# Shorter loads for every ninth tile of attention, and the first expert's weights queued behind the attention's last load

## The chip, the cores and the metric

The kernel runs on one core of one Trainium2 chip. The metric is the device time of one execution, in microseconds (us). The kernel before takes 399.77 us, the median of three runs (399.61 to 401.5).

The engines are named as the profile names them: PE (TensorE, the matrix products), PEld (its weight loads, which overlap PE), DVE (VectorE), ACT (ScalarE), POOL (GpSimd) and SP (SyncE, which here only issues DMAs). SBUF is the memory on the chip, PSUM the banks that PE writes.

## The reference

Decayed attention without a softmax, and behind it a layer of experts of which each token uses at most one:

```python
scores = scale * np.matmul(q, k.transpose(0, 1, 3, 2))     # q, k, v: 8 x 8 x 576 x 64
Dmat   = np.where(rel >= 0, gamma[:, None, None] ** rel[None, :, :], 0.0)
attn   = np.matmul(scores * Dmat[None, :, :, :], v)
x      = attn.transpose(0, 2, 1, 3).reshape(4608, 512)

do_compute = x @ w_skip > 0
xc     = x[do_compute]
logits = xc @ w_gate                                       # 8 experts
e_idx  = np.argmax(logits, axis=1)
gate_w = softmax(logits)[np.arange(len(xc)), e_idx]
for e in range(8):
    h       = np.maximum(xc[e_idx == e] @ w1[e], 0.0)      # 512 -> 1024
    y[e_idx == e] = gate_w[e_idx == e, None] * (h @ w2[e]) # 1024 -> 512
out = x;  out[do_compute] = xc + y
```

## The kernel before

**Attention (about 0 to 156 us).** It goes over 36 tiles of 128 tokens (NT = 36, number g), nine (NQ) for each pair of sequences. The first eight of the nine hold 64 tokens of each of two sequences' blocks; the ninth (g % NQ == HALF, so g = 8, 17, 26, 35) holds the last 64 rows of both. A tile's input is one buffer `u_g` of four parts of 128x512 numbers: parts 0 and 1 are columns of q and k, part 2 rows of v, part 3 rows of k. There are UBUFS = 5 such buffers. `load_half(g, s)` (L501) fetches two parts by one 512 KB DMA on SP's queue: the first half (s = 0) of tile g+4 is written behind `values` of tile g-1, which frees the buffer (L852); the second half (s = 2) of tile g+3 a step later, behind the last product of a block on PE (L836).

For each tile PE makes `scores` (L552, results psc and psq in PSUM), DVE and ACT multiply them by the decays (`decay`, L573: sq at L578, u in place at L581, ACT's copy at L585), POOL multiplies the rows of k by a table (`keys`, L587: kn) and the rows of v by another (`rows_of`, L604: vs), PE makes the running state of a sequence from kn and u or vs (`state`, ps_s at L626) and the tile's result from scores and state (`values`, pxt at L651 and L675, which DVE scales into xt at L687). `stage_c` (L689) turns xt by PE into px; ACT copies it to xn and sends it to the output. `keys` returns at once for the ninth tile: a sequence's state isn't needed behind its last rows, so part 3 of tiles 8, 17, 26 and 35 is loaded and never read. Before the loop `keys(0)` stands twice (L788 and L822) and writes the same values.

**Routing.** Every four tiles, `logits_a` and `logits_b` make the gate logits (PE pl, ACT lt, PE pn, DVE lg at L717); px, pl and pn share one PSUM bank. `route_a` and `route_b` (DVE, L187 to L258) find each token's expert, gate weight and rank; `slot_match` (DVE r, L266) and `slot_add` (PE ps_m, L271) add them to the table of slots. This is done in six groups of tiles (GROUPS, 8 8 8 4 4 4). Behind the third, the first expert is chosen, and SP reads its number into a register (L359). Behind the fourth, `close_first` fixes the first 256 tokens of that expert (CUT); POOL gathers their rows by two indirect DMAs (xg, L341), and `turn_early` and `up_early` start this expert's first products (ph_early) while the last two groups are still being routed. DVE's rl (L405) belongs to the slots' table, which the experts' gathers need.

**The first expert's weights.** A chunk of weights is 512 KB. It is loaded into one of four raw buffers (tag "w", `load_w`, L157), and split into a rounded part and a rest: ACT casts whi, and a subtraction makes wlo. For the first expert's first five chunks (AHEAD = 5) this is `weights()` (L744): each call starts the load of the next chunk, n, and splits chunk n-2, with ACT's cast at L753 and POOL's subtraction in four pieces at L758. It is called at the end of each step g once the expert's register is there (from g = 29 on), and then in a loop behind the last tile until five chunks are split. All other chunks are split by `split_w` (ACT L169, DVE L170) in the experts' part.

**Experts (about 180 to 395 us).** PE multiplies almost without a pause.

The order on PE is written out by hand (`in_turn` interleaves the products of several steps); the order on the other engines is made by the scheduler from the order of the code, from when things are ready and from `add_manual_dep`, with the operations of `weights()` kept in program order.

Of the kernel before, what the change touches and what calls it, by code (L numbers as in the profile page):

```python
# [22 lines left out]
NTOK, DM, NE, DF = B * S, H * D, 8, 1024  # L23
P = 128
NT = NTOK // P
HALF = S // P * 2
NQ = HALF + 1
# [21 lines left out]
UAHEAD = UBUFS - LAG  # L49
# [36 lines left out]
def kernel(  # L86
# [10 lines left out]
    nc = tc.nc  # L97
# [15 lines left out]
    def keep_up(n):  # L113
        for _ in range(n):
            nc.tensor.matmul(ps_m, warm[:, :P], warm, start=True, stop=True)
# [41 lines left out]
    def load_w(e, f, regs):  # L157

        t = wpool.tile([P, 2, NCC, P], F32, tag="w", name=f"w_{e}_{f}", bufs=4)
        marks["load"] = nc.sync.dma_start(t.rearrange("p m c i -> p (m c i)"), w[bass.ds(regs[e], 1), f].rearrange("o p c -> (o p) c"))  # L160
        return t

    def parts(t):
        return [wpool.tile([P, 2, NCC, P], F32R, tag=n, name=f"{n}_{t.name}") for n in ("whi", "wlo")]
# [277 lines left out]
    wq, hs, marks = {}, {}, {}  # L442
    regs = []
# [38 lines left out]
    with ExitStack() as actx:  # L482
# [16 lines left out]
        u_t = {}  # L499

        def load_half(g, s, after=None):  # L501
            if s == 0:
                u_t[g] = ap.tile([P, 4, NPR, P], F32, tag="u", name=f"u_{g}", bufs=UBUFS)
            half = nc.sync.dma_start(
                u_t[g][:, s : s + 2].rearrange("p s a i -> p (s a i)"),
                qkv[g, s // 2],
            )
            if after is not None:
                tc.add_manual_dep(
                    half.ins,  # L510
                    after.name,
                    mybir.DependencyInfo(mybir.DependencyClass.Sync, mybir.DependencyReason.DATA),
                    reason="the second half begins behind a block of products",
                )
# [5 lines left out]
        def last_product():  # L520
            return next(i for i in reversed(nc.cur_bb.bb.instructions) if i.engine == mybir.EngineType.PE)
# [30 lines left out]
        def scores(g):  # L552

            u = u_t[g]
            psc_t[g] = [
                pp.tile([P, NPR, P], F32, tag=f"sc{g % 2}", name=f"psc_{g}"),
                pp.tile([P, NPR, D], F32, tag="sc2", name=f"psq_{g}"),
            ]
            for a in range(NPR):
                for c in range(2):  # L560
                    q = first(g) if c == 0 else slice(D, P)
                    for j in range(2):
                        nc.tensor.matmul(  # L563
                            psc_t[g][c][halves[1 - j ^ c], a, : q.stop - q.start],
                            u[halves[j], 1 - j, a, c * D : (c + 1) * D],
                            u[halves[j], j, a, q],
                            start=a == 0,
                            stop=a == NPR - 1,
                            skip_group_check=True,
                        )  # L570
                yield
# [15 lines left out]
        def keys(g):  # L587
            i = g % NQ
            if i == HALF:
                return  # L590
            kn_t[g] = ap.tile([P, NPR, P], F32, tag="kn", name=f"kn_{g}")
            k = TK + i // 2 * 2
            nc.gpsimd.tensor_tensor(  # L593
                kn_t[g].rearrange("p a (j i) -> p a j i", j=2),
                u_t[g][:, 3].rearrange("p a (j i) -> p a j i", j=2),
                tt_sb[:, k : k + 2, :].rearrange("p j a -> p a j").unsqueeze(3).broadcast_to([P, NPR, 2, D]),
                ALU.mult,
            )
# [44 lines left out]
        def second(g):  # L643

            last = g % NQ == HALF
            px_t[g] = pp.tile([P, NPR, P], F32, tag="xt", name=f"pxt_{g}", bufs=2)
            for a in range(NPR):
                for n in range(1 + last):
                    for j in range(2):
                        h = halves[j]  # L650
                        nc.tensor.matmul(  # L651
                            px_t[g][h, a, D:],
                            st_t[g][h, a, :] if n else u_t[g][h, 2, a, j * D : (j + 1) * D],
                            u_t[g][h, j, a, D:] if n else sc_t[g][h, a, :],
                            start=a == 0 and n == 0,
                            stop=False,
                            skip_group_check=True,
                        )
                yield

        def in_turn(*products):

            products = list(products)
            while products:
                products = [p for p in products if next(p, p) is not p]
# [76 lines left out]
        chunks = []  # L742

        def weights():  # L744

            if not regs:
                return
            n = len(chunks)
            chunks.append(None)
            if 0 <= n - 2 < AHEAD:  # L750
                t = chunks[n - 2]
                hi, lo = wq[0, n - 2] = parts(t)
                tc.keep_in_program_order(nc.scalar.copy(hi, t))  # L753
                behind = ranked[-1] if len(ranked) == len(GROUPS) - 1 else None
                for m in range(2):
                    for c in range(0, NCC, NCC // 2):
                        some = lambda x: x[:, m, c : c + NCC // 2]
                        piece = nc.gpsimd.tensor_tensor(some(lo), some(t), some(hi).bitcast(F32), ALU.subtract)  # L758
                        tc.keep_in_program_order(piece)
                        if behind is not None:  # L760
                            tc.add_manual_dep(
                                piece.ins,
                                behind.ins.name,
                                mybir.DependencyInfo(mybir.DependencyClass.Sync, mybir.DependencyReason.DATA),
                                reason="VectorE's operations on the gates go first",
                            )
                            behind = None
            if n < AHEAD:
                chunks[n] = load_w(0, n, regs)

        def slots(t):
            slot_match(t)
# [12 lines left out]
        mctx = tc.manual_schedule(engines={mybir.EngineType.PE})  # L785
        mctx.__enter__()
        lt = None
        keys(0)  # L788
        def route(b):

            if (b + 1) * NB not in starts:
                return False
            k = starts.index((b + 1) * NB) - 1
            ra = route_a(starts[k], GROUPS[k])
            more = lambda: route_b(ps_m, k == 0, k > KCUT, k == KRANK, *ra)
            todo.append((False, g + 1 + (k <= KCUT), more))
            cnt = ra[4]
            if k == KONE:
                todo.append((True, 0, lambda: choose_first(ps_m, cnt)))
                todo.append((False, 0, lambda: regs.append(expert_reg(lead_id[0:1, 0:1]))))  # L800
            for t in range(starts[k], starts[k + 1]):
                todo.append((False, 0, lambda t=t: slots(t)))
            if k == KCUT:
                todo.append((True, 0, lambda: close_first(ps_m, cnt, starts[k + 1] * P)))
            if k == KRANK:
                counted.append(cnt)
            return True
# [20 lines left out]
        for g in range(NT):  # L828
            ahead = g + 1 < NT
            last = g - LAG  # L830
            products = [scores(g + 1)] if ahead else []
            if last >= 0 and last % NQ < HALF:
                products.append(second(last))
            in_turn(*products)
            if g and g + UAHEAD - 1 < NT:
                load_half(g + UAHEAD - 1, 2, last_product())  # L836
            if last >= 0 and last % NQ == HALF:
                in_turn(second(last))
            if ahead:
                decay(g + 1)  # L840
            if g + 2 < NT:
                keys(g + 2)
            if ahead:
                rows_of(g + 1)
            if g < len(NKEEP):
                keep_up(NKEEP[g])
            if g < NQ - 1 and g % 2 == 0:
                table(g // 2 + 1)
            logits(g)
            in_turn(state(g), *([values(last)] if last >= 0 else []))  # L850
            if g + UAHEAD < NT:
                load_half(g + UAHEAD, 0)  # L852
            if last >= 1:
                stage_c(last - 1)
            routing(0 if g == NT - 1 else 3 if g < starts[KCUT + 1] else 8)
            weights()
        g = NT
        if LAG:
            in_turn(second(NT - 1))
# [498 lines left out]
```

## Time and profile before

| what | us |
|---|---|
| median of three runs | 399.77 |
| lowest to highest | 399.61 to 401.5 |
| the profiled execution | 403.33 |
| its span, first to last instruction | 401.5 |
| PE busy in the span | 377.0 (94%) |
| DVE busy | 283.1 (71%) |
| ACT busy | 181.2 (45%) |
| POOL busy | 150.1 (37%) |

The profiled execution lies 3.6 us over the median; 1.8 us of its time lie outside its span. Moments below are microseconds from the start of the span. Over the whole span the DMA engines moved 105.62 MB at a mean of 263 GB/s, and SP's queue carried 84.95 MB of them. The mean granted clock of TensorE was 0.984 of full speed.

In a timeline a line holds the start, the duration, the engine and code line, the operation, and `out<-in` by the program's names; the bracket at its end holds how long the engine was idle before, and what released it. `x4` at its end says that four like instructions are drawn together.

### The profile page before, as it was taken

The page shows a single profiled execution, that of the slowest core. Times are in us where ns is not written, and L with a number is a line of the kernel's source. Part 1 is how long each engine was busy: PE and PEld are TensorE (multiplying, and loading weights), DVE is VectorE, ACT ScalarE, POOL GpSimd, SP SyncE. Part 2 cuts the span into 40 slices and gives each one's busy share as a digit, 9 for nine tenths or more (in the row PEclk, how much of TensorE's full clock was granted, in tenths as well). Part 3 has the DMA queues.
Part 4 walks back from the last instruction along what each step waited for, and adds up shares of the span by engine and source line. Part 5 has one row for each costly group of instructions (what it writes and reads, how often), then busy time and mean ns, then how long its engine had stood idle before and what let it go on. Part 6 is the DMA issues. An engine that isn't in the chain of part 4 may idle for free.

```text
span 401.5 us, 12406 instructions
## 1 busy us (share of the span) xinstructions
PE 377.0 (94%) x4904; PEld 341.1 (85%) x4904; DVE 283.1 (71%) x623; ACT 181.2 (45%) x367; POOL 150.1 (37%) x210
## 2 busy tenths in 40 slices
PE   7899989979998897999999999999999999999991
PEld 3678768767877785979999999999999999999990
DVE  2666586587589878977766756768867677687752
ACT  2454546345535476115534443554545535555220
POOL 5975655545575489151044102220321212001122
PEclk9999999989999989999999999999999999999996
DMA  8999999987999997226886877779797897867211
GB/s 308 357 345 325 378 331 307 371 312 234 344 343 307 334 359 227 81 67 209 301 264 183 327 230 247 265 211 348 250 301 245 280 341 266 255 244 229 86 54 57
DMA packets 47579, 105.62 MB, mean 263 GB/s; under 512 B 6158, under 2 KB 19598, under 8 KB 47518
## 3 DMA queue, kind: packets, MB, share of 16 engines
q1 hardware_dynamic: 38526, 84.95, 62.5%
q0 software_dynamic: 3232, 9.99, 7.8%
q10 hardware_dynamic: 5760, 9.85, 6.6%
q8 instruction: 40, 0.66, 0.7%
q14 instruction: 21, 0.17, 0.1%
HBM read 83.77 MB, written 21.41 MB: 262 GB/s over the span
## 4 chain that ended last, share of the span: by engine, by line
PE 59%; DMA 18%; issue 10%; DVE 5%; POOL 2%; ACT 2%; SPq 1%; POOLq 0%; ACTq 0%; DVEq 0%
PE py L454 16%; PE ph L454 15%; DMA out<-rs,sidx 8%; PE pxt L675 6%; DMA u<-qkv 5%; PE ps_s L626 4%; PE psc L563 4%; PE px L693 3%; PE pxt L651 2%; PE pl L701 2%; DMA xg<-out,gidx 2%; DMA out<-xn 2%; DMA hop<-xg 1%; PE psq L563 1%; POOL kn L593 1%
## 5 line engine op out<-in xcount | busy, mean ns | idle before, releaser
L170 DVE TENSOR_TENSOR wlo_w<-w,whi_w 128x1024 fp32r<-128x1024 f32 x59 | 72.0, 1225 | 41.8 <-ACT whi_w L169 41.1
L169 ACT CAST whi_w<-w 128x1024 fp32r<-128x1024 f32 x59 | 61.6, 1050 | 34.4 <-PE py L454 31.7
L454 PE MATMUL py<-hlo,whi_w 128*128 128x344 f32 (+6 forms) x224 | 68.0, 303 | 0.2
L454 PE MATMUL ph<-xhi,whi_w 128*128 128x344 f32 (+6 forms) x224 | 67.9, 303 | 0.0
L454 PE MATMUL ph<-xlo,whi_w 128*128 128x344 f32 (+6 forms) x224 | 67.7, 302 | 0.0
L454 PE MATMUL ph<-xhi,wlo_w 128*128 128x344 f32 (+6 forms) x224 | 67.7, 302 | 0.0
L454 PE MATMUL py<-hhi,wlo_w 128*128 128x344 f32 (+6 forms) x224 | 67.7, 302 | 0.0
L454 PE MATMUL py<-hhi,whi_w 128*128 128x344 f32 (+6 forms) x224 | 67.6, 302 | 0.0
L993 POOL DMA_INDIRECT out<-rs,sidx x17 | 20.8, 1224 | 90.9 <-DVE rs L992 89.3
L593 POOL TENSOR_TENSOR kn<-u,tt_sb 128x512 f32<-128x512 f32 x33 | 35.2, 1065 | 45.6 <-DMA u<-qkv 18.4
L675 PE MATMUL pxt<-u,vs 128*64 128x128 f32 (+1 forms) x576 | 50.2, 277 | 0.7 <-issue 0.7
L585 ACT COPY u<-psc 64x256 f32<-64x256 f32 x64 | 23.5, 367 | 57.1 <-DVE u L581 51.7
L612 POOL TENSOR_TENSOR vs<-u,tt_sb 64x256 f32<-64x256 f32 x72 | 44.6, 620 | 11.0 <-PE psq L563 2.4
L462 ACT ACTIVATE hhi<-ph 128x344 fp32r<-128x344 f32 (+8 forms) x61 | 25.9, 425 | 46.3 <-PE ph L454 46.0
L581 DVE TENSOR_TENSOR u<-psc,mt_sb 64x256 f32<-64x256 f32 x72 | 30.2, 420 | 22.5 <-PE pxt L651 8.7
L626 PEld LDWEIGHTS ps_s<-u,kn 128*64 128x64 f32 x512 | 32.5, 142 | 12.8 <-issue 7.0
L454 PEld LDWEIGHTS py<-hlo,whi_w 128*128 128x128 f32 x224 | 42.2, 188 | 1.0 <-DVE hlo L463 0.9
L626 PE MATMUL ps_s<-u,kn 128*64 128x64 f32 x512 | 39.7, 233 | 3.3 <-POOL vs L612 1.7
L454 PEld LDWEIGHTS ph<-xhi,whi_w 128*128 128x128 f32 x224 | 42.2, 188 | 0.1
L454 PEld LDWEIGHTS ph<-xlo,whi_w 128*128 128x128 f32 x224 | 42.2, 188 | 0.1
L454 PEld LDWEIGHTS py<-hhi,whi_w 128*128 128x128 f32 x224 | 42.2, 188 | 0.0
L454 PEld LDWEIGHTS ph<-xhi,wlo_w 128*128 128x128 f32 x224 | 42.2, 188 | 0.0
(217 smaller groups left out, 808.0 us busy)
## 6 DMA issues: line engine op xcount, KB each, us to landing
u<-qkv SPq DMA_DIRECT2D x72, 512.0 KB, 5.7
w<-w SPq DMA_DIRECT2D x64, 512.0 KB, 5.2
out<-xn ACTq DMA_DIRECT2D x36, 256.0 KB, 5.7
hop<-xg SPq DMA_DIRECT2D x12, 256.0 KB, 4.9
xh<-hop SPq DMA_DIRECT2D x48, 64.0 KB, 4.5
hopy<-yp SPq DMA_DIRECT2D x24, 128.0 KB, 4.5
yr<-hopy SPq DMA_DIRECT2D x6, 512.0 KB, 4.5
hop_r<-xr SPq DMA_DIRECT2D x2, 256.0 KB, 6.0
```

The costliest lines, as they stand in the source:

```text
L169: nc.scalar.copy(hi, t)
L170: nc.vector.tensor_tensor(lo, t, hi.bitcast(F32), ALU.subtract)
L454: nc.tensor.matmul(ps, x, y, start=first and n == 0, stop=last and n == 3 * len(terms) - 1)
L462: nc.scalar.activation(hi, ph, AF.Relu)
L563: nc.tensor.matmul(psc_t[g][c][halves[1 - j ^ c], a, : q.stop - q.start], u[halves[j], 1 - j, a, c * D : (c + 1) * D], u[halves[j], j, a, ...
L581: nc.vector.tensor_tensor(u_t[g][h, j, :, :D], near[h, :, :D], mt_sb[h].unsqueeze(1).broadcast_to([D, NPR, D]), ALU.mult)
L585: nc.scalar.copy(u_t[g][h, j, :, D:], near[h, :, D:])
L593: nc.gpsimd.tensor_tensor(kn_t[g].rearrange("p a (j i) -> p a j i", j=2), u_t[g][:, 3].rearrange("p a (j i) -> p a j i", j=2), tt_sb[:, k ...
L612: nc.gpsimd.tensor_tensor(vs_t[g][h, j], u_t[g][h, 2, :, j * D : (j + 1) * D], tt_sb[h, TV + g % NQ // 2, :].unsqueeze(2).broadcast_to([D, ...
L626: nc.tensor.matmul(ps_s[halves[j], i % 2, a, :], kn_t[g][:, a, j * D : (j + 1) * D], u_t[g][:, 2, a, j * D : (j + 1) * D], start=i == 0 an ...
L675: nc.tensor.matmul(pxt[halves[j], a, q], vs_t[g][:, j, a, :], u_t[g][:, j, a, q], start=False, stop=a == NPR - 1, skip_group_check=True,)
L993: done = nc.gpsimd.indirect_dma_start(out=out, out_offset=bass.IndirectOffsetOnAxis(ap=idx, axis=0), in_=rs[:n], in_offset=None, bounds_ch ...
```

## The change

1. The second half of tiles 8, 17, 26 and 35 fetches one part (rows of v) instead of two: 256 KB for 512 KB, in pieces of 2 KB per partition for 4 KB. Part 3 of these buffers stays as it was, and nobody reads it.
2. Each load of a half is kept in `marks["u"]`, and a weights' load of `weights()` is written to be issued behind the last such load.
3. The `keys(0)` that stands ahead of `route` is gone: POOL makes 32 kn for 33.
4. `weights()` is called in the last four steps only: twice at g = 32, and once at g = 33, 34 and 35; the loop behind the tiles does the rest. Before, it was called in each step from g = 29 on.

```diff
         def load_half(g, s, after=None):
             if s == 0:
                 u_t[g] = ap.tile([P, 4, NPR, P], F32, tag="u", name=f"u_{g}", bufs=UBUFS)
-            half = nc.sync.dma_start(
-                u_t[g][:, s : s + 2].rearrange("p s a i -> p (s a i)"),
-                qkv[g, s // 2],
+            n = 1 if s and g % NQ == HALF else 2
+            half = marks["u"] = nc.sync.dma_start(
+                u_t[g][:, s : s + n].rearrange("p s a i -> p (s a i)"),
+                qkv[g, s // 2, :, : n * DM],
             )
...
             if n < AHEAD:
-                chunks[n] = load_w(0, n, regs)
+                with tc.issue_after(marks["u"].ins):
+                    chunks[n] = load_w(0, n, regs)
...
         lt = None
-        keys(0)
+
         def route(b):
...
             routing(0 if g == NT - 1 else 3 if g < starts[KCUT + 1] else 8)
-            weights()
+            for _ in range((0, 1, 2)[(g + UAHEAD >= NT) + (g + UAHEAD == NT)]):
+                weights()
```

On **SP's queue**, around the last loads of attention. The names u_2508, u_2624 and u_2715 are tiles 33, 34 and 35 (u_2506, u_2620, u_2709 in the changed kernel), w_0 to w_3 the first expert's chunks, ISA and TENSOR_LOAD the register's instructions. Before:

```order
L504 DMA u_2508<-qkv 128x1024
L359 TENSOR_LOAD lead_id
L160 ISA
L160 DMA w_0_2541<-w 128x1024
L504 DMA u_2508<-qkv 128x1024
L504 DMA u_2624<-qkv 128x1024
L160 ISA
L160 DMA w_1_2655<-w 128x1024
L504 DMA u_2624<-qkv 128x1024
L504 DMA u_2715<-qkv 128x1024
L160 ISA
L160 DMA w_2_2741<-w 128x1024
```

And now:

```order
L505 DMA u_2506<-qkv 128x1024 x2
L505 DMA u_2620<-qkv 128x1024 x2
L505 DMA u_2709<-qkv 128x1024
L505 DMA u_2709<-qkv 128x512
L359 TENSOR_LOAD lead_id
L160 ISA
L160 DMA w_0_2821<-w 128x1024
L160 ISA
L160 DMA w_1_2823<-w 128x1024
```

w_0, w_1 and w_2 moved from between the halves of tiles 33 to 35 to behind all of them, and the register's read with them.

On **POOL**, from tile 33's vs to the end of the split (kn and vs as above, xg the two gathers, wlo the subtractions). Before:

```order
L612 TENSOR_TENSOR vs_2711<-u_2508,tt_sb 64x256 x2
L758 TENSOR_TENSOR wlo_w_0_2541_2735<-w_0_2541,whi_w_0_2541_2734 128x256 x4
L593 TENSOR_TENSOR kn_2777<-u_2624,tt_sb 128x512
L612 TENSOR_TENSOR vs_2797<-u_2624,tt_sb 64x256 x2
L758 TENSOR_TENSOR wlo_w_1_2655_2837<-w_1_2655,whi_w_1_2655_2836 128x256 x4
L612 TENSOR_TENSOR vs_2903<-u_2715,tt_sb 64x256 x2
L341 DMA xg_130<-out,gi_2938 128x512 x2
L758 TENSOR_TENSOR wlo_w_2_2741_2949<-w_2_2741,whi_w_2_2741_2948 128x256 x4
```

And now:

```order
L613 TENSOR_TENSOR vs_2705<-u_2506,tt_sb 64x256 x2
L594 TENSOR_TENSOR kn_2762<-u_2620,tt_sb 128x512
L613 TENSOR_TENSOR vs_2782<-u_2620,tt_sb 64x256 x2
L613 TENSOR_TENSOR vs_2883<-u_2709,tt_sb 64x256 x2
L341 DMA xg_130<-out,gi_2918 128x512 x2
L759 TENSOR_TENSOR wlo_w_0_2821_2929<-w_0_2821,whi_w_0_2821_2928 128x256 x4
L759 TENSOR_TENSOR wlo_w_1_2823_3021<-w_1_2823,whi_w_1_2823_3020 128x256 x4
L759 TENSOR_TENSOR wlo_w_2_2935_3056<-w_2_2935,whi_w_2_2935_3055 128x256 x4
```

The subtractions of w_0 and w_1 moved from between the tiles to behind the gathers: five stand there in a row, where there were three.

On **ACT**, from the last casts of the split to the first hhi (whi the casts, x the copies for the early products, xn and lt as above, hhi the first expert's activations). Before:

```order
L753 CAST whi_w_4_2955_3073<-w_4_2955 128x1024
L174 CAST x_131<-pt_early_3106 128x2x256
L174 CAST x_131<-pt_early_3113 128x2x256
L695 COPY xn_3125<-px_3120 128x512
L169 CAST whi_w_5_3271_3421<-w_5_3271 128x1024
L696 DMA out<-xn_3125 128x512
L710 COPY lt_3133<-pl_3128 128x512
L695 COPY xn_3140<-px_3135 128x512
L696 DMA out<-xn_3140 128x512
L462 ACTIVATE hhi_0_3165<-ph_early_3164 128x256
```

And now:

```order
L174 CAST x_131<-pt_early_3090 128x2x256
L174 CAST x_131<-pt_early_3097 128x2x256
L696 COPY xn_3109<-px_3104 128x512
L697 DMA out<-xn_3109 128x512
L754 CAST whi_w_3_3027_3112<-w_3_3027 128x1024
L754 CAST whi_w_4_3062_3119<-w_4_3062 128x1024
L711 COPY lt_3131<-pl_3126 128x512
L169 CAST whi_w_5_3269_3419<-w_5_3269 128x1024
L696 COPY xn_3138<-px_3133 128x512
L697 DMA out<-xn_3138 128x512
L462 ACTIVATE hhi_0_3163<-ph_early_3162 128x256
```

The casts of w_3 and w_4 moved from ahead of the x copies to right ahead of lt, and that of w_5 to between lt and the last xn. The order on PE is unchanged, and that on DVE but for a place or two of two hlo operations.

## Rows read from the trace of the kernel before

**Rows 1.** Windows: busy us (and count) of PE, PEld, DVE, ACT, POOL; clock; DMA share; GB/s.

```profile
50.00:90.00 40.00, 36.28 (x845) 29.96 (x841) 29.47 (x81) 17.86 (x45) 22.05 (x32) 0.97 0.95 330
...
130.00:145.00 15.00, 13.27 (x290) 11.14 (x289) 12.05 (x41) 8.07 (x18) 8.39 (x12) 0.89 0.98 360
139.20:142.60 3.40, 3.40 (x35) 3.07 (x36) 1.32 (x3) 2.48 (x5) 2.53 (x4) 0.50 1.02 411
240.00:380.00 140.00, 139.81 (x1021) 138.92 (x1020) 102.82 (x155) 68.26 (x118) 23.12 (x21) 1.00 0.79 257
```

**Rows 2.** Waits from 8 to 150 us: who for whom, us, times, longest.

```profile
POOL kn L593 <- DMA u<-qkv: 15.3, 9, 4.2
```

**Rows 3.** Timeline of POOL and PE at tiles 10 and 29.

```profile
41.71 1.06 POOL L593 TENSOR_TENSOR kn<-u,tt_sb 128x512 f32<-128x512 f32 x1 [1.30 <-DMA u<-qkv]
...
44.15 0.34 PE L675 MATMUL pxt<-u,vs 128*64 128x64 f32 x4 [0.70 <-issue]
...
118.45 1.06 POOL L593 TENSOR_TENSOR kn<-u,tt_sb 128x512 f32<-128x512 f32 x1 [1.33 <-PE px L693]
...
121.00 0.34 PE L626 MATMUL ps_s<-u,kn 128*64 128x64 f32 x4 [1.10 <-POOL vs L612]
```

**Rows 4.** Page, DMA issues: count, KB each, us from issue to landing.

```profile
u<-qkv SPq DMA_DIRECT2D x72, 512.0 KB, 5.7
```

**Rows 5.** Timeline of PE and POOL at tiles 32 and 33.

```profile
137.54 0.27 PE L563 MATMUL psq<-u 64*64 64x64 f32 x2 [1.23 <-DVE sq L578]
...
138.11 1.06 POOL L593 TENSOR_TENSOR kn<-u,tt_sb 128x512 f32<-128x512 f32 x1 [4.16 <-DMA u<-qkv]
...
139.19 0.48 PE L626 MATMUL ps_s<-u,kn 128*64 128x64 f32 x4 [0.50 <-POOL kn L593]
```

**Rows 6.** Timeline of POOL at the start.

```profile
9.78 1.06 POOL L593 TENSOR_TENSOR kn<-u,tt_sb 128x512 f32<-128x512 f32 x1 [1.18 <-DMA u<-qkv]
```

**Rows 7.** Timeline of POOL from 146 to 162 us.

```profile
146.43 2.78 POOL L758 TENSOR_TENSOR wlo_w<-w,whi_w 128x256 fp32r<-128x256 f32 x4
149.29 1.34 POOL L612 TENSOR_TENSOR vs<-u,tt_sb 64x256 f32<-64x256 f32 x2
150.92 1.24 POOL L341 DMA_INDIRECT xg<-out,gi  x1 [0.29 <-POOL vs L612]
...
153.48 8.27 POOL L758 TENSOR_TENSOR wlo_w<-w,whi_w 128x256 fp32r<-128x256 f32 x12
```

**Rows 8.** Timeline of DVE from 147 to 167 us.

```profile
147.86 1.40 DVE L328 SCALAR_TENSOR_TENSOR idf<-raw 128x16 f32<-128x16 f32 x1
...
153.63 0.67 DVE L200 SCALAR_TENSOR_TENSOR mks<-lg,oh 128x32 bf16<-128x32 f32 x1
...
159.33 2.45 DVE L237 TENSOR_SCALAR sm<-sm 128x4 f32<-128x4 f32 x1
...
163.51 0.19 DVE L257 TENSOR_TENSOR mk<-prb,mks 128x32 f32<-128x32 f32 x1
...
163.96 1.37 DVE L266 TENSOR_SCALAR r<-iota,trank 128x384 bf16<-128x384 f16 x4
...
165.58 0.30 DVE L717 TENSOR_REDUCE lg<-pn 128x36 f32<-128x144 f32 x1
...
166.91 0.16 DVE L237 TENSOR_SCALAR sm<-sm 128x4 f32<-128x4 f32 x1
```

**Rows 9.** Timeline of ACT at 160 us.

```profile
160.04 0.59 ACT L710 COPY lt<-pl 128x512 f32<-128x512 f32 x1 [0.24 <-PE pl L701]
161.38 0.59 ACT L695 COPY xn<-px 128x512 f32<-128x512 f32 x1 [0.74 <-PE px L693]
```

**Rows 10.** Timeline of PE between attention and the experts.

```profile
151.46 0.66 PE L693 MATMUL px<-ident,xt 128*128 128x128 f32 x4 [0.81 <-DVE lg L717]
...
166.07 0.47 PE L271 MATMUL ps_m<-mc,r 128*128 128x40 bf16 x12
...
171.88 0.17 PE L282 MATMUL ps_m<-cb,ones 128*128 128x8 bf16 x1 [0.29 <-DVE rl L405]
```

**Rows 11.** The weights' DMAs from 130 to 165 us: landing times, from the tile w.

```profile
DMA to landing us min/median/max: 4.0/5.9/8.9
```

## The prediction

> **What bounds the kernel now.** I read the windows by stage first, to see which resource has no slack where the change works. In attention neither has much: from 50 to 90 us PE is busy 36.28 of 40 us and the DMA engines 0.95 of the time at 330 GB/s; from 130 to 145 us PE 13.27 of 15 and the DMA engines 0.98 at 360 GB/s. From 240 to 380 us PE is busy 139.81 of 140 us and the DMA share is 0.79 [rows 1]. So nothing that happens behind some 180 us can gain, and whatever is gained or lost in attention or in the transition (150 to 180 us) goes one for one into the time, as the experts follow without a gap.
>
> Next, the waits: in attention POOL's kn waits 15.3 us in nine places for a tile's DMA, 4.2 at most [rows 2]. That says that loads are late, not that it costs: POOL is off the path unless PE waits for kn or vs. So the third view is the timeline of PE, gap by gap, each followed back to its releaser. Of PE's gaps between 8 and 150 us only a few lead to a DMA; they are small, and are in rows 3 and 5. The fourth view is the transition, where DVE's small gate operations, POOL's subtractions and ACT's copies take turns on the path [rows 7 to 10].
>
> **Part 1, the shorter loads.** A load of 512 KB takes 5.7 us from issue to landing [rows 4], several being under way at once. At 330 GB/s [rows 1] the 256 KB left out of each of four loads are 0.79 us of the queue, so at most 4 x 0.79 = 3.2 us if the stage went strictly by bytes. It doesn't: PE is the nearer bound. The late loads that PE feels are those of tile 10 (kn waited 1.30 for its DMA at 41.71, PE 0.70 at 44.15) and tile 29 (kn at 118.45, PE 1.10 at 121.00) [rows 3]. Both tiles are loaded in the wake of a ninth tile (8 and 26), so loads that end 0.79 earlier there meet them in part. Of the 0.70 I take 0.5 and of the 1.10, whose last releasers are POOL's own work and PE, 0.4: **-0.9**. Bounds: 0 (the saved time only lets the queue run empty, as the next load waits for a buffer that PE frees) and 0.70 + 1.10 = -1.8; -3.2 belongs to a rival.
>
> **Part 2, the weights' loads go behind the attention's.** w_0, w_1 and w_2 no longer share the queue with tiles 33 to 35. The wait that points to them is the longest one: kn of tile 33 at 138.11 waited 4.16 for its DMA. But PE's gap there, 1.23 at 137.54, was ended by DVE's sq, not by the load; only the 0.50 at 139.19 was ended by that kn [rows 5]. An earlier landing lets kn run some 3 us earlier, beside DVE's gate operations of another group, and part 4 shows what POOL does to those. I take **0**; bounds -0.5 (the second gap goes) and +1.5 (two POOL operations of about a us fall on DVE's chain just ahead of sq, a cost the size of the 1.40 us in rows 8).
>
> **Part 3, one kn less.** kn of tile 1 at 9.78 had been waiting 1.18 for its DMA [rows 6], so POOL had time to spare behind the doubled `keys(0)`: **0**. The cover is that wait; without it the price would be one kn, 1.06 us.
>
> **Part 4, the split behind the gathers.** This is where the sum turns. POOL's subtractions of w_0 and w_1 (2.8 us each in four pieces of 0.7, the second at 146.43 [rows 7]) leave the last tiles and stand behind the gathers, five in a row.
>
> First what that gives. DVE's idf took 1.40 us at 147.86, for a 128x16 operation whose like take 0.19, and ended when the subtraction beside it did at 149.21; it stands in the chain of DVE work ahead of lg, for which PE waited 0.81 at 151.46 [rows 7, 8, 10]. That gap goes, -0.8, and the gathers come earlier: vs of tile 35 at 149.29 started when w_1's subtraction ended, and the first gather at 150.92 stood behind it [rows 7]. With both gone I put the start of the subtractions at 151.8 for 153.48, the 1.4 that idf lost and a little of POOL's own.
>
> Then what it costs. Twelve pieces took 8.27 us, 0.69 each [rows 7]; twenty take 13.8, so POOL's stream ends near 165.6, where it ended at 153.48 + 8.27 = 161.75. Beside it run DVE's operations for the fifth group. Operations that touch only SBUF wait there for a piece: mks took 0.67, and sm at 159.33 took 2.45 where its twin at 166.91, with POOL idle, took 0.16 [rows 8]. Reductions and those that read PSUM were not held, nor was r at 163.96 after the stream. In before, only the first of nine such operations behind 159.33 was held, since the stream ended under it; now all nine lie inside it. At one piece each they take 9 x 0.72 = 6.5 us from 159.33 - 0.8 = 158.5 to 165.0. Two short ones (some 0.19 each, as mk at 163.51) and r's 1.37 bring the last r to 166.8, for 163.96 + 1.37 = 165.33 before: **+1.5**. Who waits: PE's additions of r at 166.07, with 0.74 us in hand, and behind r on DVE the next lg (165.58 before), which starts the last group's chain, for whose end (rl) PE waited 0.29 already at 171.88 [rows 8, 10]. So the delay comes out at 171.88 nearly whole. Bounds: +0 (the operations slip in between the pieces and keep the 0.16 of the twin) and the operation at 159.33 being held to the end of the stream: 165.6 plus what followed it before, 165.33 - 161.78 = 3.55, is 169.15, +3.8.
>
> ACT meets the same point. Two casts now stand ahead of lt at 160.04, and w_4's load waits for a raw buffer, that is for the end of wlo_0 at about 154.6; a weights' load takes 4.0 to 8.9 us to land [rows 11], so w_4 is there at 158.6 to 160, w_5, behind wlo_1, some 2.8 us later, and its cast stands ahead of the last xn at 161.38, which waited for PE 0.74 [rows 9]. That makes PE's early products late by +0.2 to +1.4, less the 0.8 gained: it reaches 171.88 beside DVE's +1.5, not on top of it. The later of the two counts, and I keep +1.5.
>
> A rule of the Trainium skill speaks to the size of this. First the trace: sm's 2.45 us went past the ends of three pieces of 0.7 [rows 8]. The page "SBUF — State Buffer", section "SBUF: two separate sides", says that VectorE and GpSimd share a port pair as an exclusive lock, held for a whole instruction, and that the loser blocks fully; by it a DVE operation would wait for one piece at most, which is the +1.5, while the row says that the next piece can win again, which is the way to the +3.8. The trace does not agree with the short wait everywhere, so both are kept.
>
> **Sum.** Against the profiled execution: 403.33 - 0.9 + 0 + 0 + 1.5 = 403.9. That execution lies 3.6 us over the median; the same changes on the median give 399.77 + 0.6 = **400.4 us**. A measurement of this kernel can tell about 0.5%, 2.0 us, from no change, so the forecast is "no change that shows".
>
> **The rivals.**
>
> *F, faster: attention goes by its DMA after all.* For it: a DMA share of 0.98 and 360 GB/s from 130 to 145 us, and 4.16 us of waiting at tile 33 [rows 1, 5]. Two ways lead to about the same size: all four loads count by bytes, -3.2; or the lone load at tile 29 gives -0.9, the gap at 139.19 goes (-0.5), and with it the stretch from 139.20 to 142.60 at a granted clock of 0.50, the lower of the two levels, where half of 3.4 us is lost (-1.7) [rows 1], -3.1. With DVE slipping between POOL's pieces, part 4 gives 0: 399.77 - 3.1 = 396.7. Against it: PE's gaps that a DMA ended come to 1.8 us, and the 1.23 that ended right ahead of the slow stretch was DVE's.
>
> *S, slower: DVE is held to the end of POOL's stream.* The place is sm at 159.33, the price +3.8 as above; it decides as soon as r's end is later than PE's 166.07 + 0.74, that is when DVE is let go behind 163.3 or so. PE then stands some 3 us still, and a pause of PE of 1.23 us at 137.54 was followed by 3.4 us at the lower clock [rows 1, 5], another +1.7: 399.77 - 0.9 + 3.8 + 1.7 = 404.4. For it: the 2.45 us. Against it: mks, 0.67, was let in after one piece [rows 8].
>
> *N, the shorter loads give nothing.* The next load is written only when PE frees a buffer, and the saved 0.79 us is idle queue: 399.77 + 1.5 = 401.3.
>
> That the change doesn't do what it says is ruled out by the order, where the loads and calls stand as announced.
>
> **How the numbers follow.** Forecast 0.44, F 0.24, S 0.23, N 0.09. The predicted time is the forecast's, 400.4. Its own range, by the bounds of parts 1, 2 and 4, is 398 to 402.5. Of F's and S's cases I leave out the ends: 397.0 to 404.4 leaves out a tenth on each side. Faster than 397.8 are F and a little of the forecast, 0.26; slower than 401.8 are S, a quarter of N and the upper end of the forecast, 0.30; between them lies 0.44.
>
> **What would show it.** In the changed profile: the halves of tiles 8, 17, 26 and 35 as 256 KB loads; PE's gap near 44 and 121 smaller by about a half (part 1), or as large (N), or attention's end earlier by 3 us (F); kn of tile 33 without its wait for a DMA; idf at 0.2 us and no gap ahead of px near 151; the subtractions as one block of about 13.8 us ending near 165.6; gate operations of 0.7 us each beside it, the last r some 1.5 us later against the early products, and PE waiting 1.5 to 2 us for DVE's rl near 172 (S: one operation of 4 us or more, and a stretch of halved clock). I am wrong if attention's end moves by over 1 us either way, or if DVE's chain ends as early as before though POOL's block is as long as I say.

## The result: slower, and where the time went

The changed kernel takes 406.02 us (median of 22 runs) against 400.75 for the kernel before; the ratio is 1.0112, with a 95% interval of 1.0091 to 1.0133. That is 4.5 us slower (5.3 us by the plain medians), and a second set of runs gave 1.0108 (1.0053 to 1.0162). The forecast was 400.4 us and a range from 397.0 to 404.4. (The ratios leave out runs that lie over 1.5% above the fastest of the same kernel, which takes out more of a kernel whose runs lie far apart, five of twelve for e2 and six of twelve for e7 below, so the plain medians of all runs stand beside them.)

The two profiled spans, 401.5 and 403.5 us, are only 2.0 us apart, and that misleads. Each must be cut at a point that both kernels share. I cut at PE's gap ahead of tile 33's psq and at PE's step that waits for rl [rows 5, 10]. Up to the first cut PE needed 136.31 us in the profile of before and 132.45, 138.49 and 135.50 in three profiles of the changed kernel: this part differs by up to 6 us between executions of one kernel. From the first cut to the second it took 35.57 us before and **40.86, 40.24 and 40.44** after. These 4.7 to 5.3 us are as much as the whole loss. Behind the second cut the changed kernel's profiles take 0.1 to 0.6 us more than that of before.

The timeline of PE in the changed kernel shows the four places at which PE waits (columns as in rows 10; lines from L504 on have moved by one):

```profile
135.14 0.27 PE L564 MATMUL psq<-u 64*64 64x64 f32 x2 [2.69 <-DVE sq L579]
...
158.25 0.66 PE L694 MATMUL px<-ident,xt 128*128 128x128 f32 x4 [1.82 <-ACT lt L711]
...
165.87 1.20 PE L271 MATMUL ps_m<-mc,r 128*128 128x40 bf16 x12 [0.29 <-DVE r L266]
...
173.31 0.17 PE L282 MATMUL ps_m<-cb,ones 128*128 128x8 bf16 x1 [0.29 <-DVE rl L405]
```

The first gap was 1.23 [rows 5]. The second answers to one of 0.71 us that ended at 160.68 in before. The additions of r took 1.20 us for 0.47 [rows 10], since DVE hands over one r at a time, and from there to the last line 7.44 us pass where it was 171.88 - 166.07 = 5.81.

The timeline of POOL shows what stands behind the first place, and the new block of subtractions:

```profile
131.66 1.06 POOL L594 TENSOR_TENSOR kn<-u,tt_sb 128x512 f32<-128x512 f32 x1 [1.55 <-DMA u<-qkv]
132.79 1.34 POOL L613 TENSOR_TENSOR vs<-u,tt_sb 64x256 f32<-64x256 f32 x2
...
149.40 13.78 POOL L759 TENSOR_TENSOR wlo_w<-w,whi_w 128x256 fp32r<-128x256 f32 x20
```

And the timeline of DVE shows what POOL does to it at both:

```profile
131.73 1.02 DVE L240 CAST cp<-gt 128x4 bf16<-128x4 f32 x1
...
132.98 0.48 DVE L242 CAST cp<-gt 128x4 bf16<-128x4 f32 x1
...
133.69 0.48 DVE L244 CAST cp<-gt 128x4 bf16<-128x4 f32 x1
...
145.05 0.21 DVE L328 SCALAR_TENSOR_TENSOR idf<-raw 128x16 f32<-128x16 f32 x1
...
149.54 0.66 DVE L200 SCALAR_TENSOR_TENSOR mks<-lg,oh 128x32 bf16<-128x32 f32 x1
...
155.78 7.45 DVE L237 TENSOR_SCALAR sm<-sm 128x4 f32<-128x4 f32 x1
...
165.40 1.37 DVE L266 TENSOR_SCALAR r<-iota,trank 128x384 bf16<-128x384 f16 x4
```

sm, an operation of 0.16 us [rows 8], took 7.45 and ended at 163.23, with POOL's block (149.40 + 13.78 = 163.18). I call this the hold. mks, at the start of the same block, waited for one piece only. idf, on the other hand, fell from 1.40 to 0.21 us, as forecast. ACT does two casts in front of lt:

```profile
155.72 1.99 ACT L754 CAST whi_w<-w 128x1024 fp32r<-128x1024 f32 x2 [0.41 <-ACT xn L696]
157.62 0.58 ACT L711 COPY lt<-pl 128x512 f32<-128x512 f32 x1
```

Behind the gaps of 2.69 and 1.82 us the granted clock fell to 0.50, the lower of the two levels, for 3.41 us each (windows, columns as in rows 1):

```profile
135.84:139.25 3.41, 3.18 (x54) 2.98 (x46) 1.67 (x4) 2.15 (x6) 0.00 (x0) 0.50 0.45 141
...
159.73:163.14 3.41, 3.23 (x16) 2.94 (x15) 3.41 (x1) 1.83 (x3) 3.41 (x6) 0.50 0.56 196
```

### The profile page after: what moved, and what is told of

Its sections match the earlier page's. It is cut to its first block, busy times and chain, and to the rows that moved or that the text cites. A ratio compares the mean times of both kernels' runs of the same rounds, so it can differ in the third digit from the quotient of the medians.

```text
span 403.5 us, 12403 instructions
## 1 busy us (share of the span) xinstructions
PE 377.0 (93%) x4902; PEld 341.1 (85%) x4904; DVE 288.8 (72%) x623; ACT 181.0 (45%) x367; POOL 147.0 (36%) x209
## 5 line engine op out<-in xcount | busy, mean ns | idle before, releaser
L996 POOL DMA_INDIRECT out<-rs,sidx x17 | 18.9, 1111 | 90.2 <-DVE rs L995 88.5
L594 POOL TENSOR_TENSOR kn<-u,tt_sb 128x512 f32<-128x512 f32 x32 | 33.9, 1060 | 45.7 <-DMA u<-qkv 19.7
L613 POOL TENSOR_TENSOR vs<-u,tt_sb 64x256 f32<-64x256 f32 x72 | 45.7, 635 | 12.0 <-ACT lt L711 2.2
L676 PE MATMUL pxt<-u,vs 128*64 128x128 f32 (+1 forms) x576 | 48.8, 273 | 0.0
L454 PEld LDWEIGHTS py<-hhi,wlo_w 128*128 128x128 f32 x224 | 42.2, 188 | 0.0
```

Of the source, the lines that this page charges most:

```text
L454: nc.tensor.matmul(ps, x, y, start=first and n == 0, stop=last and n == 3 * len(terms) - 1)
L594: nc.gpsimd.tensor_tensor(kn_t[g].rearrange("p a (j i) -> p a j i", j=2), u_t[g][:, 3].rearrange("p a (j i) -> p a j i", j=2), tt_sb[:, k ...
L613: nc.gpsimd.tensor_tensor(vs_t[g][h, j], u_t[g][h, 2, :, j * D : (j + 1) * D], tt_sb[h, TV + g % NQ // 2, :].unsqueeze(2).broadcast_to([D, ...
L676: nc.tensor.matmul(pxt[halves[j], a, q], vs_t[g][:, j, a, :], u_t[g][:, j, a, q], start=False, stop=a == NPR - 1, skip_group_check=True,)
L996: done = nc.gpsimd.indirect_dma_start(out=out, out_offset=bass.IndirectOffsetOnAxis(ap=idx, axis=0), in_=rs[:n], in_offset=None, bounds_ch ...
```

## The experiments

For every run the table has the ratio to the kernel before, the medians of that kernel and of before beside it, and from its profile: PE's gap at tile 33, from there to rl's step, DVE's sm, and the legs from the last px to the first addition of r and from there to rl's step (all us).

| kernel | ratio (95%) | medians | gap | to rl | sm | leg 1 | leg 2 |
|---|---|---|---|---|---|---|---|
| before | | 399.77 | 1.23 | 35.57 | 2.45 | 5.39 | 5.81 |
| changed | 1.0112 (1.0091, 1.0133) | 406.0, 400.8 | 2.69 | 40.86 | 7.45 | 7.62 | 7.44 |
| e6, changed again | 1.0108 (1.0053, 1.0162) | 405.1, 401.1 | 1.98 | 40.24 | 7.63 | 7.81 | 7.46 |
| e13, changed, one profile | | | 1.23 | 40.44 | 8.02 | 8.19 | 7.86 |
| e1, short loads alone | 1.0010 (0.9978, 1.0042) | 402.2, 401.1 | 1.24 | 35.66 | 2.48 | 5.37 | 5.86 |
| e2, long loads | 1.0028 (0.9991, 1.0064) | 403.8, 401.3 | 2.39 | 38.31 | 0.17 | 7.22 | 5.61 |
| e14, long loads, one profile | | | 2.16 | 39.47 | 7.79 | 7.97 | 7.45 |
| e3, lt first | 1.0019 (0.9986, 1.0051) | 402.8, 401.3 | 0.42 | 33.86 | 0.18 | 5.70 | 6.62 |
| e4, DVE free | 1.0010 (0.9976, 1.0044) | 403.3, 401.3 | 2.36 | 37.95 | 0.17 | 6.96 | 5.60 |
| e5, e3 and e4 | 1.0013 (0.9978, 1.0047) | 402.4, 401.3 | 1.96 | 36.69 | 0.17 | 5.71 | 7.26 |
| e7, kn behind gates | 0.9977 (0.9932, 1.0021) | 403.2, 401.1 | 1.23 | 38.99 | 7.61 | 7.79 | 7.86 |
| e8, all three | 0.9984 (0.9947, 1.0020) | 401.0, 401.1 | 0.39 | 34.05 | 0.17 | 5.72 | 7.17 |
| e9, e8 again | 0.9986 (0.9951, 1.0020) | 401.3, 402.2 | 1.24 | 35.14 | 0.17 | 5.70 | 7.27 |
| e10, e8 with long loads | 0.9978 (0.9939, 1.0016) | 400.6, 402.2 | 1.24 | 35.35 | 0.17 | 5.71 | 7.26 |
| e11, e8 with one block | 0.9972 (0.9934, 1.0010) | 401.6, 402.2 | 1.24 | 34.57 | 0.19 | 5.69 | 6.63 |
| e12, a pause | 1.0018 (0.9985, 1.0052) | 402.8, 401.3 | 2.61 | 39.54 | 0.26 | 8.16 | 5.60 |

In e5 and e8 to e10 leg 2 is over 7 us though sm passed: PE is early there, and waits 0.7 to 0.8 us for the last group's r.

### The shorter loads alone, and the rest alone

e1 is the kernel before with part 1 of the change only:

```diff
+            n = 1 if s and g % NQ == HALF else 2
             half = nc.sync.dma_start(
-                u_t[g][:, s : s + 2].rearrange("p s a i -> p (s a i)"),
-                qkv[g, s // 2],
+                u_t[g][:, s : s + n].rearrange("p s a i -> p (s a i)"),
+                qkv[g, s // 2, :, : n * DM],
             )
```

> The kernel before with only the four second halves of the ninth tiles at 256 KB; weights and all orders as before. Prediction: 0.9 us faster (0.998); rival F, by bytes: 3.2 us faster (0.992); rival N: no change (1.000); if the shorter loads are what slows the changed kernel: 1 to 2 us slower (1.003 to 1.005).

It came out at 1.0010; the interval goes from 0.9 us faster to 1.7 us slower, so it rules out the 3.2 us of F and just reaches the 0.9 us of the prediction. The two gaps on PE that part 1 of the prediction meant to shorten are both there in e1's timeline, at 1.18 and 1.03 us for 0.70 and 1.10 [rows 3]:

```profile
44.57 0.28 PE L676 MATMUL pxt<-u,vs 128*64 128x64 f32 x2 [1.18 <-issue]
...
119.79 0.30 PE L627 MATMUL ps_s<-u,kn 128*64 128x64 f32 x3 [1.03 <-POOL vs L613]
```

These gaps come and go with the execution: the first profile of the changed kernel has none at the first place and 0.34 us at the second, that of e6, the same kernel, 1.18 and 1.00, and that of e10, with long loads, 0.57 and 0.34. So no single profile can tell what the shorter loads do to them; the times have to.

e2 is the other side, the changed kernel with `n = 2` for the new line of `load_half`.

> The changed kernel with the ninth tiles' second halves at 512 KB again, as before. The changed kernel itself is 1.1% (4.5 us) over the kernel before. If the shorter loads give the 0.9 us of the prediction, this run is 5.4 us over it (1.0135); if attention goes by bytes (the rival's 3.2 us), 7.7 us (1.019); if they give nothing, 4.5 us (1.011).

By the medians it lies 2.5 us over before, where the changed kernel lies 4 to 5.3 over. Its twelve runs go from 400.3 to 409.35 us, too far apart to show that it is faster than the changed kernel. In its profile sm passed in 0.17 us, in an execution that took 407.5 us; a second profile of the same kernel (e14, below) has the hold, in one that took 403.18. So whether sm is held differs from one execution to the next, the loads don't decide it, and the time of a single execution says little about it, as it holds the varying part ahead of the first cut too. e10 against e9, the same pair without the losses, gives 0.9978 and 0.9986: again nothing for the loads.

### Three moves, alone and together

e3 writes ACT's lt copy ahead of the casts of w_3 and w_4:

```diff
+        logits(NT + LAG)
         while len(chunks) < AHEAD + 2:
             weights()
-        logits(NT + LAG)
```

> The changed kernel with one code block moved: the last group's lt copy is written ahead of the casts of w_3 and w_4, so that ACT does it first (order on POOL, PE and SP as in the changed kernel). Theory POOL (the last r, held back by the 7.45 us of DVE's sm beside POOL's subtractions, sets the time): PE's gap of 1.82 us ahead of px shrinks to about 0.7, but PE then waits some 2 us more for r, and the time stays within 0.5 us of the changed kernel (4 to 5 us over before). Theory ACT (the gap of 1.82 us and the 3.4 us at half clock that follow the two casts set the time): 1.1 + 1.7 = 2.8 us come back, 1.7 us over before (1.004).

e4 makes the subtractions of w_2, w_3 and w_4 wait for the fifth group's mc, with no order changed (`rest` is the loop over the four pieces as it stood in `weights`):

```diff
+                if n - 2 < 2:
+                    rest(t, hi, lo, ranked[-1] if len(ranked) == len(GROUPS) - 1 else None)
+                else:
+                    later.append((t, hi, lo))
...
         routing(1)
+        for t in later:
+            rest(*t, marks["mc"])
         up_early(0)
```

> The changed kernel with POOL's subtractions of w_2, w_3 and w_4 made to wait until DVE has written the fifth group's mc; the order on every engine is that of the changed kernel. Both theories: sm takes 0.2 us for 7.45, the last r of the fifth group ends near 160 for 166.8. Theory POOL: PE no longer waits for r and rl (0.28 + 3 x 0.07, the additions of r 0.3 us for 1.2, later some 0.3 more): 1.5 to 1.8 us come back, 2.8 us over before (1.007). Theory ACT: PE is late by its own gap and clock, 0.3 us come back, 4.2 us over before.

e5 has both.

> e3 and e4 together. If both chains end at the same place and each hides the other, this gives more than the two apart: 1.1 (gap) + 1.7 (half clock) + 1.5 (waits for r and rl) = 4.3 us come back, about 0.2 us over before (1.0005), against 0 for e3 and 1.5 for e4. If the loss lies ahead of the transition (the gap of 2.69 us at 135.14, where kn of tile 33 runs earlier), the time stays over 2 us above before.

e3 came out at 1.0019, e4 at 1.0010 and e5 at 1.0013: by the medians each move alone gives back some 2 to 4 us of the 4 to 5.3, and both together little more. So the two theories, one chain each, were too simple; the moves overlap in what they give back, and these runs don't say how. e4 does what both said (sm 0.17, and PE doesn't wait for r), and its leg 2 returns from 7.44 to 5.60; its gap ahead of px stays at 1.82, and leg 1 at 6.96, with a stretch at half clock in it. e3 takes that gap away (0.71, as in before), and its profile has no stretch at half clock there: the granted clock is 1.00 from 134.78 to 168.65. Its timelines of PE and ACT show the gap and the new order:

```profile
156.33 0.44 PE L694 MATMUL px<-ident,xt 128*128 128x128 f32 x2 [0.71 <-ACT lt L711]
...
162.03 0.47 PE L271 MATMUL ps_m<-mc,r 128*128 128x40 bf16 x12
```

```profile
155.69 0.58 ACT L711 COPY lt<-pl 128x512 f32<-128x512 f32 x1 [1.19 <-PE pl L702]
156.17 2.00 ACT L754 CAST whi_w<-w 128x1024 fp32r<-128x1024 f32 x2
```

But e3's sm passed too, at 0.18 us, though the block of subtractions was left as it was; I had expected the hold. What then follows is the ladder of the prediction, one piece for each operation:

```profile
154.98 0.18 DVE L237 TENSOR_SCALAR sm<-sm 128x4 f32<-128x4 f32 x1
155.19 0.18 DVE L239 RECIPROCAL gt<-sm 128x4 f32<-128x4 f32 x1
155.40 0.44 DVE L240 CAST cp<-gt 128x4 bf16<-128x4 f32 x1
155.88 0.64 DVE L241 TENSOR_TENSOR gt<-gt,cp 128x4 f32<-128x4 f32 x1
156.56 0.65 DVE L242 CAST cp<-gt 128x4 bf16<-128x4 f32 x1
```

Its r's end at 161.18, ahead of PE's 162.03. (This execution took 398.6 us, one of the two fastest of e3's twelve, so the others need not all look like it.)

e7 takes up the gap at tile 33: POOL's kn and vs of that tile wait until DVE has written the fourth group's mc (`keys` gets a second argument, which it makes kn wait for).

```diff
+            if g == 32:
+                keys(33, marks["mc"])
+                rows_of(32)
+                keys(34)
+                rows_of(33)
             for _ in range((0, 1, 2)[(g + UAHEAD >= NT) + (g + UAHEAD == NT)]):
                 weights()
```

> The changed kernel with POOL's kn of tile 33 made to wait for the fourth group's mc on DVE, so that kn and vs of tile 33 no longer run beside that group's gate operations; the order on every engine stays. In the changed kernel's profile those two made DVE's casts and subtractions take 1.02 + 0.48 + 0.48 us for 3 x 0.17, and PE waited 2.69 us for sq at 135.14 (1.23 before), with 3.4 us at half clock behind. Theory: PE's gap there falls to 1.3 us or less and the time by 1.4 us, by up to 3.1 us where the stretch at half clock goes too (ratio 0.004 to 0.008 under the changed kernel of this call). Rival: the gap is DVE's own chain and stays over 2 us, no change.

The casts L240 to L244 are back at 0.18 us each, and PE's gap is 1.23 us, the one of before:

```profile
132.85 0.27 PE L564 MATMUL psq<-u 64*64 64x64 f32 x2 [1.23 <-DVE sq L579]
...
162.75 0.24 PE L271 MATMUL ps_m<-mc,r 128*128 128x40 bf16 x3 [2.07 <-DVE r L266]
```

Its ratio is 0.9977, its median 2.1 us over before: some 2 to 3 us came back, what was expected. But the gap is not there in every execution of the changed kernel: 2.69, 1.98 and 1.23 us in its three profiles. In the third kn started at 135.90, when the last of these casts had ended at 135.76. Over all profiles the gap is at most 1.24 us in the five with kn held back (e7 to e11), and 1.96 to 2.69 in seven of the nine with the changed kernel's order of kn. The second line shows the remaining hold, for which PE, being earlier here, waits 2.07 us.

e8 has all three moves; e9 repeats it, e11 leaves e4's out again.

> The changed kernel with lt first, POOL's subtractions of w_2 to w_4 behind the fifth group's mc, and kn of tile 33 behind the fourth group's mc. The first two alone gave 1.0013 of the kernel before; if the collision at tile 33 costs 1.4 to 3.1 us, this comes out at 0.994 to 0.998, under the kernel before; if it costs nothing, at 1.001.

> The run with all three moves (lt first, subtractions of w_2 to w_4 behind the fifth group's mc, kn of tile 33 behind the fourth group's) once more, to narrow its interval: it came out at 0.9984 (0.9947 to 1.002) of the kernel before; the same is expected, 0.996 to 1.000.

> As the run beside it, but with the ninth tiles' second halves at 512 KB as before. If the shorter loads give nothing, the two agree within 0.5 us (0.001); by the prediction's 0.9 us this one is 0.002 slower; by bytes, 0.008 slower.

> The run with all three moves, but with POOL's subtractions in one block again, as in the changed kernel. If DVE's sm held to the end of that block (7.5 us) decides once ACT and tile 33 are mended, PE waits 2 us or more for the fifth group's r and this run is 2 to 3 us slower than the run with all three (about 1.005 of before); if the block is off the path, the two agree.

All four (e8 to e11) lie at 0.997 to 0.999 with intervals that reach 1.001 or 1.002: the loss is gone, and none of them is shown to be faster than the kernel before. e11's sm passed in 0.19 us, so it doesn't answer its question; it says only that a block that lets DVE in is off the path.

### What decides the hold

In all profiles so far with a hold, POOL's subtractions ran without a break; in the three where sm passed beside them (e2, e3, e11) the timeline of POOL had a pause of 0.17 us behind the first four pieces. e12 puts a pause into the changed kernel: the deferred pieces wait for the last xt, before sm begins.

```diff
             in_turn(values(NT - 1))
+        for t in later:
+            rest(*t, marks["xt"])
```

> The changed kernel with one pause in POOL's block of subtractions: those of w_1 begin only when DVE has written the last xt, some 1.6 us after those of w_0 end and some 2 us ahead of DVE's sm; the order on every engine stays. Theory PAUSE (sm is held to the end only where the block has run without a break since the gathers): sm takes 0.2 to 0.9 us for 7.5, the stretch from PE's gap at tile 33 to rl falls from 40.2 to 40.9 us to about 38, and the time by 2 us (ratio about 1.006). Rival CHANCE (a held operation gets in or not whatever went before): sm is held 5 us or more, and the time stays at 1.011 or, since the block ends 1.6 us later, gets 1 us worse.

> A third profile of the changed kernel. Theory PAUSE: the block runs 13.8 us without a break and sm is held to its end, 7 us or more. Rival CHANCE: sm passes in under 1 us in a block without a break.

> A second profile of the changed kernel with long loads, where the first showed a pause of 0.17 us behind w_0's subtractions and sm passed in 0.17 us. Theory PAUSE: sm passes if and only if that pause is there again. Rival CHANCE: sm is held though the pause is there, or passes without it.

POOL's block and DVE's sm, of e2 first, then of e14 (the same kernel), then of e12 (e13 is like e14, a block of 13.81 us and a hold of 8.02):

```profile
153.65 2.78 POOL L759 TENSOR_TENSOR wlo_w<-w,whi_w 128x256 fp32r<-128x256 f32 x4
156.60 11.15 POOL L759 TENSOR_TENSOR wlo_w<-w,whi_w 128x256 fp32r<-128x256 f32 x16 [0.17 <-ACT xn L696]
...
159.94 0.17 DVE L237 TENSOR_SCALAR sm<-sm 128x4 f32<-128x4 f32 x1
```

```profile
148.16 13.80 POOL L759 TENSOR_TENSOR wlo_w<-w,whi_w 128x256 fp32r<-128x256 f32 x20
...
154.20 7.79 DVE L237 TENSOR_SCALAR sm<-sm 128x4 f32<-128x4 f32 x1
```

```profile
153.13 2.79 POOL L751 TENSOR_TENSOR wlo_w<-w,whi_w 128x256 fp32r<-128x256 f32 x4
157.34 11.15 POOL L751 TENSOR_TENSOR wlo_w<-w,whi_w 128x256 fp32r<-128x256 f32 x16 [1.42 <-ACT whi_w L771]
...
156.51 0.69 DVE L688 TENSOR_TENSOR xt<-pxt,gt_sb 128x512 f32<-128x512 f32 x1 [0.65 <-PE pxt L676]
...
159.22 0.26 DVE L237 TENSOR_SCALAR sm<-sm 128x4 f32<-128x4 f32 x1
```

In e12 the last xt ended at 157.20 and POOL went on at 157.34, so the pause is the one that was put in, though the bracket names ACT.

The pause theory agrees with eleven profiles of eleven: sm was held in seven without a pause (before, e1, the changed kernel three times, e7, e14) and passed in four with one. It was made from eight of them; its tests are e12, e13 and e14, and only in e12, one profile, was the pause made on purpose. Two rivals bear on it. One is that sm passes where it happens to start shortly ahead of a piece's end: in the four profiles where it passed it began 0.51 to 0.59 us after the start of a piece, of the 0.69 us from one start to the next. e14 speaks against that, as its sm began 0.54 us after the start of a piece and was held. The other, not tested, is that it isn't the pause but how long POOL has run without one: sm began 1.9 to 3.3 us behind the pause where it passed, and 5.8 to 6.4 us behind the start of the block where it was held, while mks, 0.1 us into an unbroken block, waited for one piece.

e12 gave back in time what was expected or more (1.0018; 402.8 for 401.3 of before); its stretch to rl was expected at 38 and came out at 39.54, as its profile has the gap of 2.61 and stretches at half clock of 3.4 and 6.8 us as well. Why an early pause lets DVE in for the rest of the block stays open.

## Why the prediction was wrong

**Part 1, the shorter loads: -0.9, measured 0.** e1 (1.0010) and e10 against e9 show no gain, so this term is that of rival N; e1's interval alone just reaches the 0.9. The two gaps from which the term was taken vary from execution to execution, with short loads and with long ones. N's reason, that the next load only starts when PE frees a buffer, was argued and not tested.

**Part 2, the weights behind the attention: 0 with a bound of +1.5, measured +0.75 and +1.46 in two profiles of three, 0 in one.** The bound named the mechanism, and the choice between the bounds was wrong. In before, kn of tile 33 waited 4.16 us for its DMA [rows 5] and started 1.5 us after the last of DVE's casts there. That wait was a protection: with w_0 ahead in the queue, kn and vs came too late to meet DVE's gate chain. With w_0 behind them they ran at 131.66 and 132.79, right beside that chain; e7 undoes that alone, and its gap is 1.23.

**Part 3, the doubled keys(0): 0.** Not tested by itself; nothing in the profiles speaks against it.

**Part 4, first half: right.** idf fell to 0.21 us, the gap of 0.81 ahead of px near 151 went, the subtractions ran as one block of 13.78 us (forecast 13.8). Counted from tile 33's psq, the block began 1.1 to 1.7 us earlier than before (forecast 1.7).

**Part 4, the cost: here the forecast failed.** The step "at one piece each they take 9 x 0.72 = 6.5 us" was chosen for DVE; in the changed kernel's three profiles sm was held to the end of the block (7.45, 7.63, 8.02 us), the other bound. The row for that was there: 2.45 us at 159.33 [rows 8] ended at 161.78, with a block that ended at 161.75. I read it as an operation that lost to one piece after another; it is also what an operation shows that waits for the end, and behind the longer block that reading came out right. In its place the runs showed: leg 2 is 7.44 to 7.86 us with the hold and 5.60 or 5.61 without it (e2, e4, e12, ACT's order being the same), that is +1.8 us, and PE waits 0.29 to 2.14 us ahead of leg 1's end. With DVE freed by design (e4) the median is 2.0 us over before for 4 to 5.3. The step on one piece each was not wrong everywhere: mks, and the operations behind sm where sm passed, did wait for one piece at a time.

**ACT.** The size was right, in part by luck: +0.2 to +1.4 was forecast from w_4 landing at 158.6 to 160, though 4.0 to 8.9 us behind 154.6 is 158.6 to 163.5; the two casts did not wait for their loads, and with them alone the gap ahead of px grew from 0.71 to 1.82 us, +1.1, in each profile with that order. The step "it reaches 171.88 beside DVE's +1.5, not on top of it" was half right. PE's loss at px shortens its wait for r, but leg 2 comes on top, as it starts with r. And the clock was left out of this term: of the eight profiles with the gap of 1.82 six have a stretch at half clock that began within leg 1 or just before it (in e13 and e7 it came behind PE's wait of over 2 us for r).

**The sum.** At the rows' sizes: tile 33 +0.7 (the mean of three), PE's way from there to px -1.2 (the gap of 0.81 gone and smaller ones), px +1.1, leg 1 +2.2 to +2.8, leg 2 +1.6 to +2.1, together some 4.4 to 5.5 us against 4.7 to 5.3 measured between the cuts and 4.5 by the ratio. **Rival S**, given 0.23, had the mechanism (DVE held to the end of POOL's stream, then half clock). Its price came out too, 404.4 us being 4.6 over the 399.77 it was worked out from, but partly by luck: it has -0.9 for part 1, where nothing showed, and nothing for tile 33 and the casts. Its condition, that r comes later than PE wants it, was met: PE waited 0.29, 0.71 and 2.14 us for r in the three profiles. Rival F had no part: e1's interval leaves no room for 3 us.

**One piece or all.** e3's ladder shows DVE waiting for one piece at a time (0.44 to 0.65 us), the changed kernel's sm for some eleven in a row (7.45 us). The Trainium skill's page "SBUF — State Buffer", section "SBUF: two separate sides", has the port that VectorE and GpSimd share locked for a whole instruction; the first agrees with that, the second goes beyond it, and the measurement decides.

## What to carry to other kernels

A wait that costs nothing may be what keeps two engines apart: ask of each transfer that a change brings forward what its consumer will now run beside. A row in which a short operation takes as long as it is until a neighbour's block ends is to be read as "held to the end of the block", and the price of a longer block is then to be reckoned up to its end; that a neighbour waited for one piece only (mks) doesn't rule it out. Where two executions of one kernel differ by more than the effect, cut both profiles at shared points and compare the stretch between.

## What the runs showed that I had not expected

DVE's 0.16 us operation waited for up to 8.02 us beside a block of 20 POOL subtractions of 0.69 us that ran without a break, and for at most one of them where the same block had one pause of 0.17 to 1.42 us that ended 1.9 to 3.3 us earlier. And moving one ACT copy ahead of two casts (e3) gave back over half of the loss at a place where it looked like 1.1 us; in its one profile the stretch at half clock went with the gap, and the pause on POOL came.
